# Attention and two MLPs on one core: a pair's P.V. behind the next pair's third scores, decay rows in one load, new order behind the first norm, no clip of weights

## The chip, the cores and the metric

The kernel runs on one core of a Trainium2 chip. The metric is device microseconds of one execution; the time before is the median of three executions. TensorE (PE) multiplies matrices, VectorE (DVE) and ScalarE (ACT) do the elementwise work, GpSimd (POOL) a little of it and some transfers, and SyncE (SP) issues most transfers (DMA), the transposing ones among them.

## The reference

There are 4 batches, 8 heads, 576 tokens and 64 columns per head; x has 512 columns.

```
scores = q @ k.T / sqrt(D); decay = cum[:, None] - cum[None, :]   # cum = cumsum(log f)
attn   = softmax(where(causal, -1e9, scores + decay))
x      = attn @ v                                   # heads side by side: B x S x 512
xn     = (x - mean) / sqrt(var + 1e-6) * g_ln
x      = x + relu(xn @ w_ch1) @ w_ch2               # 512 -> 2048 -> 512
h      = relu(x @ w_in); u, v = h[..., :512], h[..., 512:]
vs     = einsum('ts,bsd->btd', w_spatial, norm(v)) + b_spatial
out    = (u * vs) @ w_out
```

The weights arrive as 64-bit floats.

## The kernel before

The work is cut into token blocks. Blocks 0 and 1 hold the first 128 tokens of each batch (`attention32`, float32), blocks 2 and 3 the tokens 128 to 255 (`attention1`, lines 566 to 620), blocks 4 to 7 the tokens 256 to 575 of one batch each (`attention`, lines 623 to 675). Each block's x is then normalised (`norm`) and goes through the first MLP as part of one of the groups (`mlp`): for each of 16 hidden tiles j, PE forms `ph` (L909) from `xh`, `xl` and a weight tile, ACT makes `hh` of it (L920), DVE the remainder `hl` (L924), and PE adds into `acc` (L894). Operands are pairs of 16-bit halves, so that a product takes three matmuls. Group 0 works in float32 with the narrowed weights. Behind the first MLP comes the second, from about 500 us on.

`attention` takes a block's 8 heads as 4 pairs. A pair has three score tiles of 128 queries or 64: `weights(2)` with 384 keys, `weights(3)` with 512, `weights(4)` with 576 (cut into two of 288); here they are called first, second and third scores. For each, PE makes the scores `s` (L385), DVE adds the decay `D` and finds the maximum (L411, `sd`, `st`), ACT takes the exponential with its sum (L415, L417), ACT and DVE write the two halves of P (L331, L432), and SP issues a transposing DMA of P into `PT` (L435), two for each score tile, all on one queue in a fixed order. `values` (P.V.) then multiplies `PT` by `vp`, the two halves of v, with 30 matmuls (L635) into `av`, and ACT copies that out (L640, L641). The P.V. of a pair is issued in the loop of the next one: `late` keeps it. `operands` loads `qkz` (L354 to L358) and the decay rows `D` (L362) of a pair. P.V. of the fourth pair of a block has no next pair, and stands behind the loop.

The weight tiles are loaded as 64-bit words (`raw`, three buffers) and narrowed to 32 bits during group 0 (`load_w`, `narrow`: L704 and L705 on ACT, L706 to L708 on DVE; L706 clips the magnitude). Their squares go through PE (L758), `scales` makes two factors of the sums, and `make16` splits all 16 tiles into halves at the start of group 1 (L789 on ACT, L792 on DVE).

Generators of these pieces are stepped through by one list of events (positions in numbers such as `CONV`). What they emit goes through a scheduler, which fixes the order of each engine's instructions when the program is built; `self.after(a, b)` keeps a behind b in that order. On the chip each engine works through its list in order and waits where an operand isn't there.

Of the kernel before, what the change touches and what calls it, by code (L numbers as in the profile page):

```python
# [6 lines left out]
F32 = mybir.dt.float32  # L7
# [6 lines left out]
AF = mybir.ActivationFunctionType  # L14
ALU = mybir.AluOpType
# [3 lines left out]
P = 128  # L19
B, H, S, D = 4, 8, 576, 64  # L20
DM, DFF, DF2 = 512, 2048, 1024
NK = DM // P
NF = DFF // P
NP = H // 2
# [30 lines left out]
    SPAN.append((SPAN[-1][1], SPAN[-1][1] + 2.35 / 4))  # L55
SPAN.append((SPAN[-1][1] - 0.034, SPAN[-1][1] + 0.02))
RAWAT = (-0.975, -0.974, -0.973)
CONV = (-0.6, 0.001, 0.002, 0.003, 0.004)
PACE = (1, "x3", "split", "split", "split")
LOWAT = (1, "x3", "split")  # L60
SUMS = 14
REST = 0.35
SQ = (1, 3, 4, 5, 6, 8, 9, 10, 12, 13, 14, 16)
# [21 lines left out]
def words(raw, w, dt):  # L85

    return raw.bitcast(dt).rearrange("p (n w) -> p n w", w=2)[:, :, w]


class Kernel:  # L90
# [41 lines left out]
    def setup(self):  # L132
        nc, ctx = self.nc, self.ctx
        self.cst = ctx.enter_context(self.pool("cst"))
        self.dram = ctx.enter_context(self.tc.tile_pool(name="dram", bufs=1, space=DRAM))
        cst = self.cst
        self.onesf = cst.tile([P, P], F32, name="onesf")
        nc.vector.memset(self.onesf, 1.0 / DM)
        self.ones = cst.tile([P, P], F32, name="ones")
        nc.vector.memset(self.ones, 1.0)  # L140
        self.gT = cst.tile([P, NK], F32, name="gT")
        self.eps = cst.tile([P, 1], F32, name="eps")
        nc.vector.memset(self.eps, EPS)
        self.decay1_d = self.dram.tile([B * H, 2, 3 * P], F32, name="decay1_d")
        self.decay_d = self.dram.tile([B * H, S], F32, name="decay_d")
        self.xt_d = self.dram.tile([P, NK, B, S - 512], F32, name="xt_d")
        self.x2_d = self.dram.tile([DM, NT], F32, name="x2_d")

# [92 lines left out]
    def decays16(self):  # L241


        nc, cum, n = self.nc, self.cum, B * H
        dec1 = self.dec1
        ins = nc.scalar.activation(dec1[:, 0, :P], cum[:, P : 2 * P], AF.Copy, scale=8.0)
        self.after(ins, self.marks["x3"])
        self.after(nc.scalar.activation(dec1[:, 1, P:], cum[:, : 2 * P], AF.Copy, scale=-8.0), ins)
        nc.gpsimd.dma_start(out=self.decay1_d, in_=dec1)
        row = nc.vector.tensor_scalar(out=self.lg, in0=cum, scalar1=cum[:, MID : MID + 1], scalar2=-8.0, op0=ALU.subtract, op1=ALU.mult)  # L250
        self.after(row, self.joined)
        nc.gpsimd.dma_start(out=self.decay_d, in_=self.lg)

    def gscale(self):

        nc = self.nc
        g = self.at.tile([P, DM], F32, name="gall")
        m = self.cst.tile([P, 1], F32, name="gmax")
        self.gsc = self.cst.tile([P, 2, 1], F32, name="gsc")
        self.gs = self.cst.tile([P, NK], F32, name="gs")  # L260
        load = nc.gpsimd.dma_start(out=g, in_=self.moe_g_ln.rearrange("p k -> (p k)").partition_broadcast(P))
        self.after(load, self.marks["x3"])
        biggest = nc.vector.tensor_reduce(out=m, in_=g, axis=mybir.AxisListType.X, op=ALU.max, apply_absolute_value=True)
        self.after(biggest, self.marks["third"])
        nc.vector.tensor_tensor(out=m, in0=m, in1=m, op=ALU.mult)
        self.pow2(m, self.gsc, up=UPX, k=0)
        nc.vector.tensor_scalar(out=self.gs, in0=self.gT, scalar1=self.gsc[:, 1], scalar2=None, op0=ALU.mult)
# [9 lines left out]
    def parts16(self, v, h, l, b=None):  # L277


        nc, at = self.nc, self.at  # L280
        if b is None:
            ss = at.tile([P, 1], F32, tag="vq", name="vq", bufs=4)
            sm = at.tile([P, 2, 1], F32, tag="vs", name="vs", bufs=4)
            nc.scalar.activation(h, v, AF.Square, accum_out=ss)
            pn = self.bank("s")
            nc.tensor.matmul(pn[:, :1], lhsT=self.ones, rhs=ss, start=True, stop=True)
            self.pow2(pn[:, :1], sm)
            b = 0
        else:
            sm = self.vsc  # L290
        undo, scale = sm[:, 0, b : b + 1], sm[:, 1, b : b + 1]
        nc.scalar.activation(h, v, AF.Copy, scale=scale)
        nc.vector.scalar_tensor_tensor(out=l, in0=v, scalar=scale, in1=h, op0=ALU.mult, op1=ALU.subtract)
        return undo
# [46 lines left out]
    def operands(self, b, p):  # L341

        nc, at = self.nc, self.at
        W, C = QW + 64, QW + 64 + S
        if not self.qkz:
            for i in range(BUFS["qk"]):
                self.qkz.append(at.tile([P, C], F32, name=f"qkz{i}"))
                for u in range(2):
                    c = 3 * P - 64 - 64 * u
                    nc.gpsimd.memset(self.qkz[i][64 * u : 64 * u + 64, c : c + 64], 0.0)  # L350
        qk = self.qkz[0]
        self.qkz.append(self.qkz.pop(0))
        src = self.pair_of(b)[p]
        nc.sync.dma_start(out=qk[:, W:], in_=src[:, QW:])  # L354
        nc.sync.dma_start(out=qk[:, : 2 * P], in_=src[:, : 2 * P])
        for u in range(2):
            us, c = slice(64 * u, 64 * u + 64), 2 * P + 64 * u
            nc.sync.dma_start(out=qk[us, c : c + 64], in_=src[us, 2 * P : QW])  # L358
        decay = at.tile([P, 2, S], F32, tag="D", name="D", bufs=BUFS["D"])
        r = b // 2 * 2 * H + 4 * p + b % 2  # L360
        for u in range(2):
            nc.sync.dma_start(out=decay[:, u], in_=self.decay_d[r + 2 * u].partition_broadcast(P))  # L362
        xh = at.tile([P, C], F32R, tag="xh", name="xqh", bufs=BUFS["xh"])
        xl = at.tile([P, C], F32R, tag="xl", name="xql", bufs=BUFS["xl"])
        for c in (slice(0, W), slice(W, C)):
            nc.scalar.activation(xh[:, c], qk[:, c], AF.Copy)
            nc.vector.tensor_tensor(out=xl[:, c], in0=qk[:, c], in1=f32(xh[:, c]), op=ALU.subtract)
        return xh, xl, decay
# [80 lines left out]
    def attention32(self, b, xT):  # L449
# [34 lines left out]
        def scores(p):  # L484
# [9 lines left out]
            for n, u, c in four_:  # L494
# [4 lines left out]
                ex = nc.scalar.activation(e[:, n, u], e[:, n, u], AF.Exp, bias=mn, scale=-1.0, accum_out=sm)  # L499
                if b:  # L500
                    self.after(masked, self.marks["third" if p else "w1"])
                    self.after(ex, self.marks["split"])
                if not b and p == NP - 1:
                    self.after(masked, self.drawn)
            if not b:
# [21 lines left out]
        for p in range(NP):  # L527
            for i in range(len(ahead), min(p + 2, NP) if b else NP):
# [1 line left out]
                    ahead[0] = norms(*ahead[0])  # L530
                ahead.append(scores(i))
                yield
            if b or p:
                ahead[p] = norms(*ahead[p])
            e, diag = ahead[p]
            ps, pt = bank(tags[1]), four("PT")
# [1 line left out]
                ins = mm(ps[:, n, u], lhsT=e[:, n, u], rhs=diag[:, n, u], start=True, stop=True, skip_group_check=True)  # L538
            if not b and p < NP - 1:
                self.fill(FILLS[2], ins)  # L540
            if b or p % 2:
                copied = nc.scalar.activation(pt, ps, AF.Copy)
            else:
                copied = nc.vector.tensor_copy(out=pt, in_=ps)
            if not b:
                self.done.append(copied)
                self.marks[f"PT{p}"] = copied
# [72 lines left out]
    def attention(self, b, xT, xt):  # L620
# [28 lines left out]
        for p in range(NP):  # L649
# [3 lines left out]
            yield  # L653
            if p + 1 < NP:
                ops = self.operands(b, p + 1)
            if late:
                values(*late, self.done_low)
            yield
            vr = at.tile([P, 5, P], F32, tag="vr", name="vr", bufs=BUFS["vr"])
            nc.sync.dma_start(out=vr, in_=self.v[b, :, p * P : (p + 1) * P].rearrange("(t p) d -> p t d", p=P))  # L660
            yield from self.weights(3, heads)
            yield
            vp = at.tile([P, 2, 5, P], F16, tag="vp", name="vp", bufs=BUFS["vp"])
            yield from self.weights(4, heads)
            vsc = self.parts16(vr, vp[:, 0], vp[:, 1], b)
# [25 lines left out]
    def narrow(self, raw, tmp, low=None, behind=None):  # L691
# [9 lines left out]
            nc.vector.scalar_tensor_tensor(out=b, in0=lo, scalar=29, in1=b, op0=ALU.logical_shift_right, op1=ALU.bitwise_or)  # L701
        else:

            first = nc.scalar.activation(a, words(raw, 1, F32), AF.Abs, scale=2.0**16)  # L704
            self.low = nc.scalar.activation(low.bitcast(I32), lo, AF.Copy, scale=LOW)  # L705
            clip = nc.vector.tensor_scalar(out=a, in0=a, scalar1=F64_LO * 2.0**16, scalar2=F64_HI * 2.0**16, op0=ALU.max, op1=ALU.min)  # L706
            sign = nc.vector.scalar_tensor_tensor(out=low, in0=hi, scalar=0x80000000, in1=low, op0=ALU.bitwise_and, op1=ALU.bitwise_or)
            self.joined = nc.vector.scalar_tensor_tensor(out=b, in0=b, scalar=3, in1=low, op0=ALU.logical_shift_left, op1=ALU.bitwise_or)  # L708
            if behind is not None:
                if behind is not self.marks["PT2"]:  # L710
                    self.after(clip, behind)
                self.after(sign, behind)
        return first

# [90 lines left out]
    def norm(self, x, s, y, whole, end, c):  # L805
# [33 lines left out]
            pv = self.mean(tag, sq[:, 0])  # L839
        t1 = ns.tile([P, TOK], F32, tag="t1", name="t1", bufs=2)  # L840
        nc.scalar.activation(y, pv, AF.Ln, bias=self.eps)
        nc.scalar.activation(y, y, AF.Exp, scale=-0.5)
        nc.vector.scalar_tensor_tensor(out=t1, in0=pv, scalar=EPS, in1=y, op0=ALU.add, op1=ALU.mult)
        nc.vector.scalar_tensor_tensor(out=t1, in0=t1, scalar=-0.5, in1=y, op0=ALU.mult, op1=ALU.mult)
        nc.vector.scalar_tensor_tensor(out=y, in0=t1, scalar=1.5, in1=y, op0=ALU.add, op1=ALU.mult)
# [400 lines left out]
    def run(self):  # L1246
# [85 lines left out]
            events += [(a0 + (a1 - a0) * (e + 0.5) / steps[n], 1, n) for e in range(steps[n])]  # L1332
        for g, (b0, b1) in enumerate(zip(BEGIN, BEGIN[1:])):
            events += [(b0 + (b1 - b0) * (e + 0.01) / (NF + 1), 0, g) for e in range(NF + 1)]
        events += [(CONV[j] if j < len(CONV) else G1 * (j - len(CONV) + 0.5) / (NF + 1), -1, j) for j in range(NF)]
        events += [(MAKE + 0.001 * j if j < SOON else G1 + 0.5 * (j - SOON + 0.5) / (NF + 1), -1, NF + 2 + j) for j in range(NF)]
        events += [(WSC, -1, NF + 1)] + [(VN + 0.04 * i, -1, NF) for i in range(B + 2)]
        events += [(at, -2, j) for j, at in enumerate(RAWAT)] + [(REST, -1, -1), (DEC, -1, -2)]
# [152 lines left out]
```

## Time and profile before

| | |
|---|---|
| median of 3 executions | 805.84 us (805.52 to 806.53) |
| the profiled execution | 802.58 us; its span 800.8 us, 1.78 us lie around it |
| PE busy | 760.3 us, 95% of the span |
| DVE, ACT, POOL busy | 554.3, 501.8, 66.8 us |
| PE's granted clock, mean | 0.993 of full speed |
| bytes moved | 105.96 MB, 132 GB/s |

The span runs from the first instruction to the last of the profiled execution. An engine's busy time is the sum of its instructions; PE's counts matmuls whose ends are modelled, and which overlap where they follow each other. [...]

### The profile page before, as it was taken

Reading aid. Unit: us, or ns where it says so; the run is one execution under the profiler, and the core shown is the slowest. Engines: PE = TensorE matmul, PEld = TensorE weight load, DVE = VectorE, ACT = ScalarE, POOL = GpSimd, SP = SyncE. Lnnn points to the kernel's source line nnn. Section 1 sums busy time; section 2 is a strip of 40 time slices with the busy share of each in tenths; the row PEclk is TensorE's granted clock in tenths of the full one; section 3 lists DMA queues with packets and bytes.
Section 4 is the critical chain, followed back from the end, with each engine's and each line's share of the span. In section 5 each row is a group of like instructions: output and inputs, shape, how many; then the busy total and the mean of one; then the engine's idle time right before and its main releaser. Section 6 shows DMA issues by size and latency. Waiting matters only on the chain.

```text
span 800.8 us, 16517 instructions
## 1 busy us (share of the span) xinstructions
PE 760.3 (95%) x6142; PEld 576.9 (72%) x6142; DVE 554.3 (69%) x1508; ACT 501.8 (63%) x1251; POOL 66.8 (8%) x109
## 2 busy tenths in 40 slices
PE   7899997999989999899899999999999999999998
PEld 6789886878867777688678788644447667668676
DVE  7989799485578779678877873778535562654634
ACT  6887598485477677576766763567325744656543
POOL 5000111012101011001101100100012000000000
PEclk9999999999999999999999999999999999999999
DMA  9968893376678888968996775552015230000101
GB/s 261 297 229 275 250 191 67 80 161 108 197 152 170 168 207 157 168 152 176 224 170 156 126 112 149 149 162 80 1 31 95 87 99 1 31 31 1 60 1 60
DMA packets 170963, 105.96 MB, mean 132 GB/s; under 512 B 109090, under 2 KB 156290, under 8 KB 170884
## 3 DMA queue, kind: packets, MB, share of 16 engines
q1 hardware_dynamic: 164696, 98.24, 50.7%
q0 software_dynamic: 5328, 5.16, 5.0%
q10 hardware_dynamic: 860, 1.52, 0.6%
q8 instruction: 48, 0.79, 0.4%
q14 instruction: 31, 0.25, 0.1%
HBM read 66.01 MB, written 14.72 MB: 101 GB/s over the span
## 4 chain that ended last, share of the span: by engine, by line
PE 53%; ACT 12%; DVE 12%; DMA 11%; issue 9%; SPq 1%; POOL 0%; ACTq 0%; DVEq 0%; POOLq 0%
PE ph L909 10%; PE acc L894 8%; PE pb L854 8%; PE pb L855 7%; PE pb L853 7%; DMA PT<-P 5%; PE av L635 2%; ACT wt L789 2%; DVE P L432 2%; DVE sd L411 2%; PE s L385 2%; ACT P L331 2%; DMA vr<-in_v_dram 2%; PE s L894 1%; ACT sd L415 1%
## 5 line engine op out<-in xcount | busy, mean ns | idle before, releaser
L894 PE MATMUL acc<-hh,wt 128*128 128x256 f16 (+2 forms) x960 | 197.0, 296 | 2.5 <-ACT hh L920 2.3
L909 PE MATMUL ph<-xh,wt 128*128 128x256 f16 (+1 forms) x896 | 186.8, 290 | 5.5 <-DVE hl L924 5.3
L909 PEld LDWEIGHTS <-wt 128*128 128x128 f16 x1344 | 129.4, 99 | 48.0 <-issue 10.4
L894 PEld LDWEIGHTS <-wt 128*128 128x128 f16 x1344 | 129.6, 98 | 44.0 <-issue 6.1
L909 PE MATMUL ph<-xl,wt 128*128 128x256 f16 (+1 forms) x448 | 129.5, 290 | 0.0
L894 PE MATMUL acc<-hl,wt 128*128 128x256 f16 (+1 forms) x416 | 116.0, 282 | 1.7 <-DVE hl L924 1.7
L331 ACT ACTIVATE P<-sd,st 128x384 f16<-128x384 f32 (+2 forms) x128 | 68.8, 586 | 26.1 <-DVE st L418 17.5
L920 ACT ACTIVATE hh<-ph 128x256 f16<-128x256 f32 (+2 forms) x128 | 51.0, 399 | 51.0 <-PE ph L909 50.8
L924 DVE SCALAR_TENSOR_TENSOR hl<-ph,hh 128x256 f16<-128x256 f32 (+1 forms) x112 | 51.0, 458 | 42.9 <-ACT hh L920 41.5
L415 ACT ACTIVATE sd<-sd,st 128x384 f32<-128x384 f32 (+2 forms) x80 | 54.7, 684 | 38.1 <-DVE st L411 37.9
L432 DVE SCALAR_TENSOR_TENSOR P<-sd,st,P 128x512 f16<-128x512 f32 (+1 forms) x96 | 58.2, 633 | 16.7 <-ACT P L331 15.9
L411 DVE CUSTOM_DVE_ANT_0 sd<-s,D 128x384 f32<-128x384 f32 (+2 forms) x96 | 52.4, 563 | 7.2 <-PE s L385 6.4
L945 POOL DMA_DIRECT2D x_d<-t x36 | 31.8, 1062 | 205.7 <-DVE t L941 172.3
L635 PE MATMUL av<-PT,vp 128*64 128x320 f16 (+2 forms) x480 | 32.6, 276 | 11.6 <-DMA PT<-P 11.6
L635 PEld LDWEIGHTS <-vp 128*64 128x64 f16 x480 | 25.8, 113 | 20.6 <-issue 13.0
L1221 DVE SCALAR_TENSOR_TENSOR u<-pb,wsc,u 128x288 f32<-128x288 f32 x32 | 16.0, 514 | 34.5 <-PE pb L1220 34.5
L853 PE MATMUL pb<-x2h,wil 128*128 128x288 f16 (+2 forms) x144 | 37.8, 273 | 0.0
L854 PE MATMUL pb<-x2l,wih 128*128 128x288 f16 (+2 forms) x144 | 37.7, 273 | 0.0
L855 PE MATMUL pb<-x2h,wih 128*128 128x288 f16 (+2 forms) x144 | 37.7, 273 | 0.0
L853 PE MATMUL pb<-wsh,vl 128*128 128x288 f16 x128 | 36.6, 286 | 0.2
L855 PE MATMUL pb<-wsh,vh 128*128 128x288 f16 x128 | 36.6, 286 | 0.0
L854 PE MATMUL pb<-wsl,vh 128*128 128x288 f16 x128 | 36.6, 286 | 0.0
(308 smaller groups left out, 1632.2 us busy)
## 6 DMA issues: line engine op xcount, KB each, us to landing
raw<-in_moe_w_ch_dram SPq DMA_DIRECT2D x32, 512.0 KB
D<-decay_d SPq DMA_DIRECT2D x32, 288.0 KB
vraw<-in_v_dram SPq DMA_DIRECT2D x5, 1024.0 KB
vr<-in_v_dram SPq DMA_DIRECT2D x16, 320.0 KB
x_d<-xT SPq DMA_DIRECT2D x9, 512.0 KB
x_d<-t POOLq DMA_DIRECT2D x36, 128.0 KB, 4.7
qkz<-in_qk_dram SPq DMA_DIRECT2D x16, 288.0 KB
out_dram<-o SPq DMA_DIRECT2D x32, 144.0 KB
```

Source lines behind the costliest of these rows:

```text
L331: self.nc.scalar.activation(out, in_, AF.Copy, scale=scale)
L411: self.marks["seen"] = nc.vector.tensor_tensor_reduce(out=sd[us, c0:c1], in0=banks[n if both else w][us, : c1 - c0], in1=decay[us, u, c0:c ...
L415: nc.scalar.activation(sd[:, :N], sd[:, :N], AF.Exp, bias=st[:, c : c + 1], scale=-1.0, accum_out=st[:, 4 + w : 5 + w])
L432: low = nc.vector.scalar_tensor_tensor(out=dl, in0=src, scalar=rs, in1=dh, op0=ALU.mult, op1=ALU.subtract)
L635: ins = nc.tensor.matmul(pav[us, n0:W], lhsT=vp[:, vi, kt, us], rhs=heads[u][1][:, 2 * kt + pi, n0:W], start=(kt == 0 and (vi, pi) == (0, ...
L853: first = mm(out, lhsT=al, rhs=bh, start=start, stop=False, **kw)
L854: mm(out, lhsT=ah, rhs=bl, start=False, stop=False, **kw)
L855: mm(out, lhsT=ah, rhs=bh, start=False, stop=stop, **kw)
L894: ins = nc.tensor.matmul(acc[m], lhsT=a, rhs=b, start=bank not in clear, stop=last and e == len(terms) - 1, skip_group_check=True)
L909: ins = nc.tensor.matmul(ph, lhsT=a, rhs=b, start=k == e == 0, stop=k == NK - 1 and e == len(terms) - 1)
L920: relu = nc.scalar.activation(hh, ph, AF.Relu)
L924: nc.vector.scalar_tensor_tensor(out=hl, in0=ph, scalar=0.0, in1=hh, op0=ALU.max, op1=ALU.subtract)
```

## The change

In `attention` the call of `values` for the pair before moves from ahead of `weights(3)` to behind it, so that the scheduler places it behind the third scores. In `operands` the two decay loads of a pair become one, from a table laid out by pairs. `attention1` of block 2, whose v is squared first (`b is None` in `parts16`), keeps these squares behind the last normalisation's exponential (`self.spread`, L842). The events of the weight tiles 3 and 4 and of the later ones, and the anchors that ACT's part of `narrow` stands behind (`PACE`, `LOWAT`), are other numbers. In `attention32` the norms of block 0's next pair come ahead of the copies of PT. `narrow` loses its clip L706 in the branch for the first MLP's weights; the scale of L704 becomes 2^-112 in place of 2^16.

```diff
-CONV = (-0.6, 0.001, 0.002, 0.003, 0.004)
-PACE = (1, "x3", "split", "split", "split")
-LOWAT = (1, "x3", "split")
+CONV = (-0.6, 0.001, 0.002, 0.06, 0.061)
+PACE = (1, "x3", "split", NP + 1, NP + 1)
+LOWAT = (1, "x3", "split", NP + 1, NP + 1)
@@ parts16
-            nc.scalar.activation(h, v, AF.Square, accum_out=ss)
+            self.after(nc.scalar.activation(h, v, AF.Square, accum_out=ss), self.spread)
@@ operands
-        r = b // 2 * 2 * H + 4 * p + b % 2
-        for u in range(2):
-            nc.sync.dma_start(out=decay[:, u], in_=self.decay_d[r + 2 * u].partition_broadcast(P))
+        rows = self.decay_d[b // 2 * NP + p, b % 2].rearrange("u s -> (u s)").partition_broadcast(P)
+        nc.sync.dma_start(out=decay.rearrange("p u s -> p (u s)"), in_=rows)
@@ attention32
-            if b or p:
+            if b:
                 ahead[p] = norms(*ahead[p])
...
             if not b and p < NP - 1:
                 self.fill(FILLS[2], ins)
+                ahead[p + 1] = norms(*ahead[p + 1])
@@ attention
-            if late:
-                values(*late, self.done_low)
             yield
             vr = at.tile([P, 5, P], F32, tag="vr", name="vr", bufs=BUFS["vr"])
...
             yield from self.weights(3, heads)
             yield
+            if late:
+                values(*late, self.done_low)
@@ narrow
-            first = nc.scalar.activation(a, words(raw, 1, F32), AF.Abs, scale=2.0**16)
+            first = nc.scalar.activation(a, words(raw, 1, F32), AF.Abs, scale=2.0**-112)
...
-            clip = nc.vector.tensor_scalar(out=a, in0=a, scalar1=F64_LO * 2.0**16, scalar2=F64_HI * 2.0**16, op0=ALU.max, op1=ALU.min)
...
-                if behind is not self.marks["PT2"]:
-                    self.after(clip, behind)
@@ norm
-        nc.scalar.activation(y, y, AF.Exp, scale=-0.5)
+        self.spread = nc.scalar.activation(y, y, AF.Exp, scale=-0.5)
```

PE, block 4, around the P.V. of its first pair, which is called in the loop of the second. Before, the last matmuls of that P.V. (`av`) stand straight ahead of the third scores (288 columns):

```order
L635 LDWEIGHTS vp
L635 MATMUL av<-PT,vp 64x64
L385 MATMUL s<-xqh,xql 128x288
L385 MATMUL s<-xql,xqh 128x288
L385 MATMUL s<-xqh 128x288
L385 MATMUL s_2846<-xqh,xql 128x288
L385 MATMUL s_2846<-xql,xqh 128x288
L385 LDWEIGHTS ident_1692
L385 MATMUL s_2846<-far,ident_1692 128x64
L385 MATMUL s_2846<-xqh 128x288
```

Now they stand ahead of the first scores (384 columns) of the pair after, with three matmuls of `acc` between; the third scores are 21 matmuls of `acc` ahead of the P.V.:

```order
L637 LDWEIGHTS vp
L637 MATMUL av<-PT,vp 64x64
L893 LDWEIGHTS wt
L893 MATMUL acc<-hh,wt 128x256
L893 LDWEIGHTS wt
L893 MATMUL acc<-hl,wt 128x256
L893 LDWEIGHTS wt
L893 MATMUL acc<-hh,wt 128x256
L385 MATMUL s_2885<-xqh,xql 128x384
L385 MATMUL s<-xqh,xql 128x384
```

So the third scores no longer follow the P.V., and the next pair's first scores do. ACT one pair later, before: the copies of `av` come behind the P of the second scores (`4x128`), and ahead of the next operands (L366) and of the third scores' exponential (L415, 576 columns) and P:

```order
L331 ACTIVATE P_3095<-sd,st 128x4x128
L640 ACTIVATE xT<-av,vsc 128x256
L641 ACTIVATE xt<-av,vsc 128x64
L292 ACTIVATE vp<-vr,vsc 128x640
L366 ACTIVATE xqh<-qkz_2383 128x384
L366 ACTIVATE xqh<-qkz_2383 128x576
L920 ACTIVATE hh<-ph 128x256
L415 ACTIVATE sd,st<-sd,st 128x576
L417 ACTIVATE st<-st 128x1
L331 ACTIVATE P_3118<-sd,st 128x4x128
L331 ACTIVATE P_3118<-sd,st 128x64
```

And now:

```order
L366 ACTIVATE xqh<-qkz_2367 128x384
L366 ACTIVATE xqh<-qkz_2367 128x576
L415 ACTIVATE sd,st<-sd,st 128x576
L417 ACTIVATE st<-st 128x1
L332 ACTIVATE P_3098<-sd,st 128x4x128
L642 ACTIVATE xT<-av,vsc 128x256
L643 ACTIVATE xt<-av,vsc 128x64
L332 ACTIVATE P_3098<-sd,st 128x64
L293 ACTIVATE vp<-vr,vsc 128x640
L919 ACTIVATE hh<-ph 128x256
```

The copies of `av` have moved behind the third scores' exponential, into the middle of its P. ACT near the end of group 0, before: the squares of block 2's v (L284) stand around the exponential of a norm (L842), the first exponentials of `attention1` (L590) right behind them:

```order
L920 ACTIVATE hh<-ph 128x256
L284 ACTIVATE vp,vq<-vr 128x256
L841 ACTIVATE y<-av,eps 128x256
L284 ACTIVATE vp,vq<-vr 128x256
L842 ACTIVATE y<-y 128x256
L284 ACTIVATE vp,vq<-vr 128x256
L292 ACTIVATE vp<-vr,vs 128x256
L590 ACTIVATE sd,st<-sd,st 128x256 x2
```

Now the squares follow the exponential of the second norm, after the 16-bit splits of four weight tiles (L788) and ahead of group 1's `xh`:

```order
L919 ACTIVATE hh<-ph 128x256
L841 ACTIVATE y<-y 128x256
L285 ACTIVATE vp,vq<-vr 128x256 x3
L788 ACTIVATE wt<-wt,w1c 128x512
L788 ACTIVATE wt<-wt,w2c 128x512
L919 ACTIVATE hh<-ph 128x256
L871 ACTIVATE xh<-xT,gs 128x256 x4
```

The attention of block 2 has moved from the end of group 0 into the start of group 1. On SP a pair's loads change their order (the one `D` load after the first of `qkz`, `vr` last), and the six transposes of a pair keep theirs. From the last P.V. on, PE's order is the same in both.

## Rows read from the trace of the kernel before

**Rows 1.** The page: busy us of each engine (share of the span), instructions.

```profile
PE 760.3 (95%) x6142; PEld 576.9 (72%) x6142; DVE 554.3 (69%) x1508; ACT 501.8 (63%) x1251; POOL 66.8 (8%) x109
```

**Rows 2.** PE's waits: line, what was waited for, us in total, times, longest.

```profile
PE av L635 <- DMA PT<-P: 11.6, 11, 2.2
PE ph L909 <- DVE hl L924: 5.3, 7, 1.7
...
PE s L583 <- DMA qk<-in_qk_dram: 2.0, 1, 2.0
PE s L385 <- DVE st L411: 1.7, 2, 1.0
```

**Rows 3.** Windows, PE: us, PE busy (count), granted clock, DMA share, GB/s.

```profile
117.00:200.00 83.00, 76.64 (x730) 0.98 0.55 105
...
225.00:490.00 265.00, 248.31 (x2379) 0.99 0.83 161
490.00:615.00 125.00, 124.58 (x699) 1.00 0.40 104
...
385.00:400.00 15.00, 11.88 (x119) 1.00 1.14 217
```

**Rows 4.** Timeline of PE, P.V.: start, us, instruction, idle before.

```profile
254.78 0.30 PE L635 MATMUL av<-PT,vp 128*64 128x320 f16 x1 [1.77 <-DMA PT<-P]
...
285.56 0.30 PE L635 MATMUL av<-PT,vp 128*64 128x320 f16 x1 [0.18 <-DMA PT<-P]
...
323.55 0.30 PE L635 MATMUL av<-PT,vp 128*64 128x320 f16 x1 [2.18 <-DMA PT<-P]
...
420.56 0.30 PE L635 MATMUL av<-PT,vp 128*64 128x320 f16 x1 [1.25 <-DMA PT<-P]
...
486.10 0.30 PE L635 MATMUL av<-PT,vp 128*64 128x320 f16 x1 [0.39 <-DMA PT<-P]
```

**Rows 5.** Windows of PE behind the wait at 323.55.

```profile
323.00:325.00 2.00, 1.45 (x9) 0.95 1.29 254
325.00:327.00 2.00, 2.00 (x16) 0.50 0.06 13
327.00:329.00 2.00, 2.00 (x26) 0.70 0.77 149
```

**Rows 6.** Timeline of PE: one matmul, and two that follow each other.

```profile
319.79 0.27 PE L894 MATMUL acc<-hl,wt 128*128 128x256 f16 x1
319.89 0.38 PE L894 MATMUL acc<-hh,wt 128*128 128x256 f16 x2
```

**Rows 7.** Timeline of ACT behind a P.V.

```profile
257.78 0.48 ACT L640 ACTIVATE xT<-av,vsc 128x256 f32<-128x256 f32 x1
258.15 0.31 ACT L641 ACTIVATE xt<-av,vsc 128x64 f32<-128x64 f32 x1
258.35 0.83 ACT L292 ACTIVATE vp<-vr,vsc 128x640 f16<-128x640 f32 x1
```

**Rows 8.** Timeline of SP's queue: transposes of a pair, and the next decay loads.

```profile
249.99 10.53 SPq L435 DMA_TRANSPOSE PT<-P  x6
...
261.81 1.03 SPq L362 DMA_DIRECT2D D<-decay_d  x2
```

**Rows 9.** Line 706, the clip: count, shortest/median/longest ns, first and last start.

```profile
L706 DVE TENSOR_SCALAR wt<-wt x17: 416/686/1690, 18.4 to 81.8; 128x1024 f32<-128x1024 f32 x15, 128x512 f32<-128x512 f32 x2
```

**Rows 10.** Line 284 and ACT's timeline, from block 2's squares to group 2.

```profile
L284 ACT ACTIVATE vp<-vr x8: 405/407/417, 86.4 to 143.5; 128x256 f16<-128x256 f32 x8
...
109.15 0.41 ACT L842 ACTIVATE y<-y 128x256 f32<-128x256 f32 x1
...
156.32 0.37 ACT L609 ACTIVATE xT<-av,vs 128x128 f32<-128x128 f32 x1 [0.52 <-PE av L608]
...
178.20 1.70 ACT L872 ACTIVATE xh<-xT,gs 128x256 f16<-128x256 f32 x4
```

**Rows 11.** Window of all engines at the start of group 1: PE, PEld, DVE, ACT, POOL.

```profile
100.00:130.00 30.00, 25.66 (x235) 22.09 (x234) 29.49 (x75) 28.98 (x74) 7.41 (x12) 1.00 0.76 150
```

More of the change, by code (lines that the diff above doesn't have):

```diff
@@ L144, in setup @@
         self.decay1_d = self.dram.tile([B * H, 2, 3 * P], F32, name="decay1_d")
-        self.decay_d = self.dram.tile([B * H, S], F32, name="decay_d")
+        self.decay_d = self.dram.tile([B // 2 * NP, 2, 2, S], F32, name="decay_d")
         self.xt_d = self.dram.tile([P, NK, B, S - 512], F32, name="xt_d")
@@ L251, in decays16 @@
         self.after(row, self.joined)
-        nc.gpsimd.dma_start(out=self.decay_d, in_=self.lg)
+        for i in range(2):
+            nc.gpsimd.dma_start(out=self.decay_d[:, i], in_=self.lg[i::2])
     def gscale(self):
@@ L263, in gscale @@
         biggest = nc.vector.tensor_reduce(out=m, in_=g, axis=mybir.AxisListType.X, op=ALU.max, apply_absolute_value=True)
-        self.after(biggest, self.marks["third"])
+        self.after(biggest, self.joined)
         nc.vector.tensor_tensor(out=m, in0=m, in1=m, op=ALU.mult)
@@ L501, in scores @@
                     self.after(masked, self.marks["third" if p else "w1"])
-                    self.after(ex, self.marks["split"])
+                    self.after(ex, self.done[-1])
                 if not b and p == NP - 1:
@@ L544, in attention32 @@
                 copied = nc.vector.tensor_copy(out=pt, in_=ps)
+                self.after(copied, self.masked)
             if not b:
@@ L1334, in run @@
             events += [(b0 + (b1 - b0) * (e + 0.01) / (NF + 1), 0, g) for e in range(NF + 1)]
-        events += [(CONV[j] if j < len(CONV) else G1 * (j - len(CONV) + 0.5) / (NF + 1), -1, j) for j in range(NF)]
+        events += [(CONV[j] if j < len(CONV) else max(0.061 + 0.0001 * j, G1 * (j - len(CONV) + 0.5) / (NF + 1)), -1, j) for j in range(NF)]
         events += [(MAKE + 0.001 * j if j < SOON else G1 + 0.5 * (j - SOON + 0.5) / (NF + 1), -1, NF + 2 + j) for j in range(NF)]
```

## The prediction

> **What bounds the kernel now.** I read the page's busy times first. PE is busy 760.3 of 800.8 us, DVE 554.3, ACT 501.8 [rows 1]. So a change pays where PE stands still, or where it takes work from PE, and this one takes no matmul away. The second view is PE's waits by line: the largest is that of the P.V. (L635) for the transposed P, 11 times and 11.6 us, the longest 2.2 us; then group 1's and later groups' `ph` for `hl`, 5.3 us; then single waits of some 2 us [rows 2]. The third is PE by windows: from 225 to 490 us, while the blocks 4 to 7 run, PE is idle 265 - 248.3 = 16.7 us; from 490 to 615 us, behind the last P.V., it is idle 0.4 us [rows 3]. So the wait named largest is the one that the moved P.V. can shorten, and everything behind it comes forward by as much, since PE is then full. The fourth is the timeline, where each wait has its place: those of the fourth pairs of a block (at 285.56, 420.56 and 486.10 us) last 0.18, 1.25 and 0.39 us, together 1.82; the others include the longest, 2.18 us at 323.55, and 1.77 us at 254.78 [rows 4].
>
> **The moved P.V.** The P.V. of the first three pairs of each of 4 blocks moves, 12 in all; the fourth pairs' have no next pair and stay. So 8 of the 11 waits can go, with 11.6 - 1.82 = 9.8 us [rows 2, 4]. How much later does PE now come to them? At the place shown in PE's order the third scores and 21 matmuls of `acc` are now ahead of it. Matmuls of 256 columns follow each other at 0.11 us: one alone takes 0.27 us, two take 0.38 [rows 6]. So 21 of them are 2.3 us, and the third scores, six of 288 columns at 0.11 x 288/256 = 0.12 and two small ones, about 0.8 us: 3.1 us more, and at the other eleven places 3 to 5.5 us by the same count. The transposes that it waits for become later too: the P of the third scores is now cut in two by the copies of `av`, 0.48 + 0.31 = 0.8 us [rows 7]. The margin of 3.1 - 0.8 = 2.3 us is just above the longest wait, so I take all 8 as gone: **-9.8 us**.
>
> Each wait also costs PE its overlap: the matmul ahead of it runs out its 0.27 us instead of 0.11 [rows 6], so 8 x 0.16 = **-1.3 us**. And behind the longest one the granted clock falls: 0.50 (1.2 GHz) for 2 us and 0.70 for 2 us more, after 0.95 [rows 5]; the work lost is 2 x 0.50 + 2 x 0.30 + 2 x 0.05 = 1.7 us at the full 2.4 GHz. Behind the waits up to 1.77 us no such stretch follows that I found. Without the 2.18 us wait: **-1.7 us**.
>
> **What becomes late instead.** The next pair's first scores now follow the third ones with 24 matmuls of `acc` and 30 of P.V. between. They need a bank of `s`, which DVE frees (L411). Such waits stand in the trace already: two, 1.7 us together, the longer 1.0, so the shorter 0.7 [rows 2]. None of the 12 new places need wait (0), or each like the shorter (8.4 us). I take a third of them, 4 x 0.7 = **+2.8 us**, since 24 x 0.11 + 30 matmuls of up to 320 columns leave DVE over 4 us for its four reads.
>
> Behind a fourth pair's third scores the P.V. stays close, and their P too is now cut by the copies of the third pair's `av`. Three of the four wait already [rows 4], so a delay there is paid in full: up to 4 x 0.8 = 3.2 us [rows 7], at least 0. Part of the copies runs while ACT would wait for DVE; I take a third, **+1.0 us**.
>
> **The decay rows.** 16 loads replace 32 of the same bytes; two took SP 1.03 us [rows 8], so SP gains about 0.5 us a pair. No wait of PE names D [rows 2], and a pair's six transposes alone hold the queue 10.5 us [rows 8]: 0, and at most 12 x 0.5 = 6 us if SP's queue were what makes the transposes late. [...]
>
> **The clip.** 17 instructions on DVE, 15 x 0.69 + 2 x 0.42 = 11.2 us, all between 18 and 82 us [rows 9]. They lie under PE's float32 group 0, which waits for the data of tiles and for ACT there; if the cover were gone they would be worth at most their 11.2 us. Taken as 0, with the reordered copies and tiles of that stretch.
>
> **Block 2's squares.** The first stood at 86.4 us; now they follow the second norm's exponential, at 109.15 us in the old trace [rows 10]. DVE and ACT are full in that stretch, 29.5 and 29.0 of 30 us [rows 11], so group 1 starts sooner when block 2's first three score tiles leave it: about 4 us, an estimate from counting DVE's instructions up to the first `hl`. But group 2 can't start before block 2 is through: its last copy is at 156.32 us, and `xh` for group 2 starts at 178.20 [rows 10]. In ACT's new order that copy stands behind 13 hidden tiles of group 1, where it stood behind 11; a hidden tile is 24 matmuls on PE, 2.6 us by rows 6. So 2 x 2.6 - 4 = 1.2 us later, against which the wait for `qk` of 2.0 us [rows 2] gets shorter, as that load now stands one transpose earlier on SP's queue. I take **0**, with bounds of -4 and +5.2.
>
> **Sum.** -9.8 - 1.3 - 1.7 + 2.8 + 1.0 = **-9.0 us** against the profiled 802.58 us: 793.6. The median before is 805.84, 3.3 us above the profiled execution, and I carry that over: **796.8 us**. By the bounds of the terms without the front: 805.84 - 12.8 = 793.0 and 805.84 - 12.8 + 8.4 + 3.2 = 804.6.
>
> **The rivals.**
>
> *The front gains too.* Group 1 keeps its 4 us and block 2 ends as early as before it. For it: the window of rows 11, and PE's waits of 5.3 us for `hl` and 2.0 for `qk` [rows 2], part of which go. Against it: the old 22 us from the last copy to `xh` [rows 10] are a chain of their own. Time: 796.8 - 4 = 792.8 us.
>
> *The wait only moves.* The transposes come at the pace of DMA and of SP's queue, and the P.V. meets them at its new place, or the first scores take over. For it: the DMA share is 0.83 over the 265 us and 1.14 around the waits at 389 and 392 [rows 3], 1.29 at 323 [rows 5]; at 0.83 x 265 = 220 us the transfers have a floor 45 us below, but in the stretches that count they are at it. Against it: the P.V. comes 3 us later than its data needs. Time: half to none of the gain, 801 to 806, in the middle 803.5 us. [...]
>
> *Block 2 comes late.* It is the one that ends slower. Its eight score tiles took from 86.4 to 156.3 us, 69.9 us [rows 10]. If they keep that pace from the new start, 109.15 - 4 = 105.2, the last copy comes at 175.1, 18.8 us later, and PE stands before group 2 with nothing left of group 1: 805.84 + 18.8 - 9.0 = 815.6 us. It decides from the point where that copy comes more than 9 us late, at 165.3 us. For it: few buffers, and a transpose and a P.V. in each round. Against it: in the old order 16 weight splits on ACT and DVE lay between these rounds [rows 11], and in the new one most come first.
>
> **How the numbers follow.** 0.2%, or 1.6 us, is about what a measurement of this kernel can tell from no change: 804.2 to 807.5 us. The forecast has 0.58, the front's gain 0.13, the wait that moves 0.16, block 2 late 0.13. Faster: 0.57 + 0.13 + 0.06 of the third = 0.76. Same: 0.01 + 0.10 + 0.02 of the last = 0.13. Slower: 0.11. From 789 to 805 us lie nearly all of the first two cases and most of the third, 0.81.
>
> **What would show it.** Right: PE's wait for the transposed P falls to some 3 us, all of it in fourth pairs; PE's idle time from the first scores of block 4 to the last P.V. falls from 16.7 to some 9 us; no stretch at 0.50 there; waits of the first scores for L411 rise to about 4.5 us. The front: the first `hl` of group 1 about 4 us earlier, group 2's `xh` still near 178 us. Wrong if the P.V. still waits in first to third pairs by more than 5 us together, if L411 is waited for by more than 9 us, or if group 2's `xh` moves by more than 5 us either way; a faster kernel whose P.V. waits stand unchanged would be right by accident.

## The result, and the profile after

The changed kernel takes 798.12 us (median of 8 executions, 795.07 to 799.49); the kernel before 806.18 us (median of 8, 800.35 to 808.88). The ratio is 0.990, with a 95% interval of 0.987 to 0.993. The forecast was 796.8 us. The profiled execution took 799.43 us; it is among the slower of the eight, where the profiled one of before (802.58 us) was among the faster, so the two traces differ by 3.2 us only. In what follows they say where PE waits; what an edit is worth is taken from the ratios.

The page of the changed kernel, busy us of each engine:

```profile
PE 764.0 (96%) x6142; PEld 579.3 (73%) x6142; DVE 543.1 (68%) x1491; ACT 500.3 (63%) x1251; POOL 69.4 (9%) x110
```

DVE is 11.2 us lighter than in [rows 1], which is the clip. PE's waits of the changed kernel:

```profile
PE s L385 <- DVE st L411: 8.5, 9, 2.1
PE av L610 <- DMA PT<-P: 4.2, 2, 3.2
PE av L637 <- DMA PT<-P: 3.3, 4, 1.2
PE s L585 <- DMA qk<-decay_d: 2.5, 1, 2.5
...
PE ph L908 <- DVE hl L923: 2.1, 4, 1.0
```

Against [rows 2] the P.V.'s wait for the transposed P (now L637) has gone from 11.6 us in 11 to 3.3 in 4, and these four are the fourth pairs, which didn't move. The scores' wait for the maxima L411 has grown from 1.7 us in 2 to 8.5 in 9: six of the nine stand at first scores, 7.4 us together, where one of 0.7 stood, and three at third scores, 1.1 us, where one of 1.0 stood. In `attention1` the P.V. (L610) now waits 4.2 us for the transposed P, the longest of all PE's waits, 3.2 us, among them; before it was 0.7. Windows of PE (us, PE busy, granted clock, DMA share, GB/s):

```profile
117.00:200.00 83.00, 76.48 (x676) 0.90 0.61 117
225.00:490.00 265.00, 251.37 (x2430) 0.99 0.82 163
...
120.00:128.00 8.00, 8.00 (x37) 0.50 0.63 93
...
184.00:188.00 4.00, 3.96 (x33) 0.50 0.81 120
...
392.00:394.00 2.00, 2.00 (x12) 0.50 1.25 267
```

From 225 to 490 us PE is idle 13.6 us, where it was 16.7 [rows 3]. The stretch ahead of it is new: from 117 to 200 us the granted clock is 0.90, where it was 0.98, and 8 us of it are wholly at 0.50 (matmuls of 256 columns start 0.21 us apart from 120.04 to 122.36 us, and 0.11 apart at 1.00, from 130.07 to 133.02), behind the wait of 3.2 us, and 4 us more behind the wait of 2.5 us for `qk`. The waits, and the longest of the later stages:

```profile
119.25 0.85 PE L610 MATMUL av<-PT,vp 128*64 128x128 f16 x12 [3.20 <-DMA PT<-P]
...
349.22 0.32 PE L637 MATMUL av<-PT,vp 128*64 128x320 f16 x1 [1.23 <-DMA PT<-P]
...
390.29 0.45 PE L385 MATMUL s<-xqh,xql 64*128 64x384 f32 x2 [2.10 <-DVE st L411]
```

The second line is the longest wait of a fourth pair, the third the longest of the first scores. Behind the last one the clock falls again, as it did behind the P.V.'s 2.18 us in [rows 4, 5]: the stretch at 0.50 has moved with the wait. ACT's timeline shows block 2 (beginning, last copy) and `xh` of groups 1 and 2:

```profile
98.75 0.41 ACT L841 ACTIVATE y<-y 128x256 f32<-128x256 f32 x1
99.06 0.41 ACT L285 ACTIVATE vp<-vr 128x256 f16<-128x256 f32 x1
...
101.96 1.71 ACT L871 ACTIVATE xh<-xT,gs 128x256 f16<-128x256 f32 x4
...
161.63 0.37 ACT L611 ACTIVATE xT<-av,vs 128x128 f32<-128x128 f32 x1 [0.62 <-PE av L610]
...
182.69 1.70 ACT L871 ACTIVATE xh<-xT,gs 128x256 f16<-128x256 f32 x4
```

Against [rows 10] block 2's first square comes 12.7 us later, its last copy 5.3, and group 2 starts 4.5 us later, although group 1's `xh` comes some 10 us sooner (first line at 112.5 us in the trace before).

### The profile page after: what moved, and what is told of

Read it like the earlier page. It is cut to its first block, busy times and chain, and to the rows that moved or that the text cites. A ratio compares the mean times of both kernels' runs of the same rounds, so it can differ in the third digit from the quotient of the medians.

```text
span 797.7 us, 16458 instructions
## 1 busy us (share of the span) xinstructions
PE 764.0 (96%) x6142; PEld 579.3 (73%) x6142; DVE 543.1 (68%) x1491; ACT 500.3 (63%) x1251; POOL 69.4 (9%) x110
## 4 chain that ended last, share of the span: by engine, by line
PE 51%; DVE 17%; ACT 11%; DMA 10%; issue 10%; SPq 1%; POOL 0%; ACTq 0%; DVEq 0%; POOLq 0%
PE ph L908 9%; PE pb L853 8%; PE pb L854 8%; PE pb L852 8%; PE acc L893 8%; DVE sd L411 4%; DVE P L432 3%; DMA PT<-P 3%; ACT sd L415 3%; ACT P L332 2%; DMA qkz<-in_qk_dram 2%; DVE wt L791 1%; PE s L893 1%; DMA raw<-in_moe_w_in_dram 1%; DVE xql L367 1%
## 5 line engine op out<-in xcount | busy, mean ns | idle before, releaser
L908 PE MATMUL ph<-xh,wt 128*128 128x256 f16 (+1 forms) x896 | 190.2, 294 | 2.3 <-DVE hl L923 2.1
L908 PE MATMUL ph<-xl,wt 128*128 128x256 f16 (+1 forms) x448 | 131.2, 293 | 0.0
L415 ACT ACTIVATE sd<-sd,st 128x384 f32<-128x384 f32 (+2 forms) x80 | 54.7, 685 | 51.2 <-DVE st L411 51.0
L432 DVE SCALAR_TENSOR_TENSOR P<-sd,st,P 128x512 f16<-128x512 f32 (+1 forms) x96 | 58.3, 631 | 18.1 <-ACT P L332 17.3
L411 DVE CUSTOM_DVE_ANT_0 sd<-s,D 128x384 f32<-128x384 f32 (+2 forms) x96 | 52.1, 563 | 3.5 <-PE s L385 2.8
L853 PE MATMUL pb<-gl,woh 128*128 128x288 f16 x128 | 35.6, 286 | 0.1
L854 PE MATMUL pb<-gh,woh 128*128 128x288 f16 x128 | 35.5, 286 | 0.0
```

The source lines that it names most:

```text
L411: self.marks["seen"] = nc.vector.tensor_tensor_reduce(out=sd[us, c0:c1], in0=banks[n if both else w][us, : c1 - c0], in1=decay[us, u, c0:c ...
L415: nc.scalar.activation(sd[:, :N], sd[:, :N], AF.Exp, bias=st[:, c : c + 1], scale=-1.0, accum_out=st[:, 4 + w : 5 + w])
L432: low = nc.vector.scalar_tensor_tensor(out=dl, in0=src, scalar=rs, in1=dh, op0=ALU.mult, op1=ALU.subtract)
L853: mm(out, lhsT=ah, rhs=bl, start=False, stop=False, **kw)
L854: mm(out, lhsT=ah, rhs=bh, start=False, stop=stop, **kw)
L908: ins = nc.tensor.matmul(ph, lhsT=a, rhs=b, start=k == e == 0, stop=k == NK - 1 and e == len(terms) - 1)
```

## The experiments

All ratios are to the kernel before, timed in the same session; the intervals are of 95%. The changed kernel stands at 0.990.

**1. The moved P.V. alone (e1).** On the kernel before, only the call moves:

```diff
-            if late:
-                values(*late, self.done_low)
             yield
...
             yield from self.weights(3, heads)
             yield
+            if late:
+                values(*late, self.done_low)
```

> The kernel before with the moved P.V. alone. Theory A (the move makes the gain, the rest is near nothing): 7 to 9 us below the kernel before, 797 to 799 us; P.V. waits for the transposed P fall from 11.6 us to about 3.3 us, waits of first scores for L411 rise from 1.7 us to about 8.5. Theory B (the L411 waits eat most of the move, and the front makes the other half): 3 to 5 us below, 801 to 803 us, with the same two waits. Up to the first scores of block 4 the trace is that of the kernel before under both.

797.82 us, 0.9934 (0.9904 to 0.9964): 5.3 us below the kernel before, between the two theories. Its waits:

```profile
PE s L385 <- DVE st L411: 8.9, 9, 2.1
PE av L635 <- DMA PT<-P: 5.5, 4, 3.3
```

The move takes 6.1 us from the P.V. and gives 7.2 to the scores, so by these two lines alone it gains nothing. The four P.V. waits left are fourth pairs; the longest, 3.3 us, had been 1.3 [rows 4]. In the two profiled executions the first score matmul of block 4 comes at 210.1 us before and at 206.7 here, with the same order up to there, and the last P.V. matmul at 489.1 and 484.2: of the 4.9 us between them 3.4 lie ahead of the moved work, where single executions differ by as much without a change, and 1.5 behind. So the ratio's 5.3 us (2.9 to 7.7 by its interval) is not all seen as waits in the trace, and my sum of 9.0 was too large.

**2. The P.V. back in the changed kernel (e2).** The same lines the other way.

> The changed kernel with the P.V. back in its old place. Theory A: within 2 us of the kernel before, 804 to 807 us, P.V. waits near 11 us again. Theory B: 3 to 5 us below the kernel before, 801 to 803 us.

807.28 us, 1.0053 (1.0025 to 1.0080): slower than the kernel before. So in the changed kernel the move is worth 1.5%, some 12 us, where alone it is worth 5.3. The trace shows one part of that, a longer wait in the old place:

```profile
PE av L637 <- DMA PT<-P: 15.9, 11, 4.6
```

Why it is longer there than the 11.6 us of [rows 2] these runs don't settle.

**3 and 4. Block 2's squares (e3, e4).** One takes the rule out of the changed kernel, the other puts it alone into the kernel before:

```diff
-            self.after(nc.scalar.activation(h, v, AF.Square, accum_out=ss), self.spread)
+            nc.scalar.activation(h, v, AF.Square, accum_out=ss)
```

> The changed kernel with block 2's squares free again, not behind the norm's exponential. Theory A: within 1.5 us of the changed kernel. Theory B: 2 to 4 us slower than the changed kernel. A third one, C (the late block 2 costs: a 3.2 us wait for its transposes at 119 us, 10 us at 0.50 behind it, group 2 4.5 us later): 3 to 5 us faster than the changed kernel, and group 2's xh back near 178 us.

> The kernel before with block 2's squares behind the norm's exponential, and nothing else. Theory A: within 1.5 us of the kernel before. Theory B: 2 to 4 us faster. C: 2 to 5 us slower, with group 2's xh at 180 to 185 us instead of 178.

Without the rule: 789.07 us, 0.9827 (0.9789 to 0.9865), about 6 us by the ratios below the changed kernel. The rule alone: 807.04 us, 1.0047 (1.0023 to 1.0072), 3.8 us above the kernel before. Theory C holds on both sides; without the rule the gain is even above its 3 to 5 us. ACT's timeline without the rule (e3), last copy of block 2 and `xh` of group 2:

```profile
153.85 0.37 ACT L611 ACTIVATE xT<-av,vs 128x128 f32<-128x128 f32 x1 [1.50 <-PE av L610]
...
175.24 1.71 ACT L871 ACTIVATE xh<-xT,gs 128x256 f16<-128x256 f32 x4
```

And with the rule alone (e4):

```profile
180.88 1.70 ACT L872 ACTIVATE xh<-xT,gs 128x256 f16<-128x256 f32 x4
```

Group 2 starts at 175.2, 178.2 [rows 10], 180.9 and 182.7 us: without the rule, before, with the rule alone, in the changed kernel. In e3 the window that stood at 0.90 in the changed kernel is at 1.00; with the rule alone (e4) it is at 0.96, before at 0.98 [rows 3]:

```profile
117.00:200.00 83.00, 80.88 (x785) 1.00 0.53 113
```

**5 to 7. What else the change holds (e5, e6, e7).** All three on e3: the clip back (with the scale 2^16 and its place in the order), the old numbers of the weight tiles, and two decay loads:

```diff
...
+            clip = nc.vector.tensor_scalar(out=a, in0=a, scalar1=F64_LO * 2.0**16, scalar2=F64_HI * 2.0**16, op0=ALU.max, op1=ALU.min)
...
```

```diff
-CONV = (-0.6, 0.001, 0.002, 0.06, 0.061)
+CONV = (-0.6, 0.001, 0.002, 0.003, 0.004)
...
```

```diff
-        rows = self.decay_d[b // 2 * NP + p, b % 2].rearrange("u s -> (u s)").partition_broadcast(P)
-        nc.sync.dma_start(out=decay.rearrange("p u s -> p (u s)"), in_=rows)
+        for u in range(2):
+            nc.sync.dma_start(out=decay[:, u], in_=self.decay_d[b // 2 * NP + p, b % 2, u].partition_broadcast(P))
```

> The changed kernel without the rule on block 2's squares (789.1 us), and with the clip back. Theory C1 (the clip's 11 us of DVE lay ahead of group 1 and its absence brings the front forward): 793 to 797 us, group 1's xh 3 to 4 us later than 107.8 us. C2 and C3 (it is the order of the weight tiles, or the joined decay loads): within 1.5 us of 789.

> The same base with the old events and anchors of the weight tiles (CONV, PACE, LOWAT, the max in the events). C2 (the new order of the tiles brings the front forward): 793 to 797 us, group 1's xh 3 to 4 us later than 107.8 us. C1 and C3: within 1.5 us of 789.

> The same base with two decay loads of a pair again. C3 (half as many loads on SP's queue bring the transposes forward): 792 to 795 us, P.V. waits and waits of the first scores for L411 grow by 2 us or more together. My prediction's 0: within 1.5 us of 789, the same waits.

The old tile numbers: 789.01 us, 0.9824 (0.9794 to 0.9855), no difference. The clip: 792.62 us, 0.9870 (0.9832 to 0.9909), about 3.5 us slower, though the interval meets that of e3; and C1's sign for it is not there, as `xh` of group 1 doesn't come later (107.8 us in e3):

```profile
106.72 1.70 ACT L874 ACTIVATE xh<-xT,gs 128x256 f16<-128x256 f32 x4
```

Two loads: 794.82 us, 0.9893 (0.9862 to 0.9925), about 5 us slower; the interval is apart from that of experiment 6 in the same session. The waits of e7:

```profile
PE s L385 <- DVE st L411: 9.0, 8, 2.1
PE av L637 <- DMA PT<-P: 4.6, 4, 2.0
```

and of e3:

```profile
PE s L385 <- DVE st L411: 8.2, 8, 2.1
...
PE av L637 <- DMA PT<-P: 3.2, 4, 1.2
```

The two waits together are 2.2 us longer, as C3 had it; that is less than half of the 5 us.

**8. The remainder of the operands on GpSimd (e8).**

```diff
-            nc.vector.tensor_tensor(out=xl[:, c], in0=qk[:, c], in1=f32(xh[:, c]), op=ALU.subtract)
+            nc.gpsimd.tensor_tensor(out=xl[:, c], in0=qk[:, c], in1=f32(xh[:, c]), op=ALU.subtract)
```

> The same base with the remainder of the next pair's operands (L367, 1.3 us a pair) on GpSimd instead of VectorE. Theory D (VectorE's work between a pair's third scores and the next pair's first is what those wait for): waits of the first scores for L411 fall from 8.2 to under 4 us and the time by 3 to 6 us, 783 to 786 us. Rival E (GpSimd is slower at it, and the first scores wait for xql instead): the sum of both waits stays, 788 to 792 us.

799.12 us, 0.9958 (0.9930 to 0.9986), slower than both theories had it. The waits for L411 stay (7.8 us), 1.5 us for `xql` are added, `ph` waits 5.5 us for `hl` where it waited 2.5 in e3, and some of DVE's instructions slow down beside GpSimd's work:

```profile
365.81 3.44 POOL L367 TENSOR_TENSOR xql<-qkz,xqh 128x384 fp32r<-128x384 f32 x2 [2.17 <-ACT xqh L366]
...
...
367.91 1.89 DVE L432 SCALAR_TENSOR_TENSOR P<-sd,st,P 128x512 f16<-128x512 f32 x1
```

L432 with 512 columns takes 760 ns on average in e3 from 225 to 490 us and 903 here; this one takes 1.89 us beside GpSimd's two of 3.44 together. So the experiment doesn't show what these waits would be with L367 off DVE and DVE as fast as before.

**9 and 10. Joined loads and no clip, each with the moved P.V. on the kernel before (e9, e10).** The edits are those of the change.

> The kernel before with the moved P.V. and the joined decay loads, nothing else. If the joined loads are worth 5 us wherever they stand (theory L): 0.986 to 0.989 of the kernel before, against 0.9934 with the moved P.V. alone; P.V. waits and L411 waits together 2 us or more below the 14.4 us of that one. If they are worth nothing, as I had put it: 0.992 to 0.995.

> The kernel before with the moved P.V. and without the clip, nothing else. If VectorE's 11 us of clip delay the start of group 1 (theory K): 0.988 to 0.991 of the kernel before, and group 1's xh before 109 us instead of 111.3. If the clip lies under PE's work, as I had put it: 0.992 to 0.995 and the same xh.

The loads: 795.24 us, 0.9896 (0.9854 to 0.9939), 3 us below e1, with intervals that overlap; its profiled execution, 802.97 us, was the slowest of six by 5.7 us and doesn't serve for waits. No clip: 792.22 us, 0.9843 (0.9805 to 0.9880), 7 us below e1, with intervals apart, and below the range of theory K too. `xh` of groups 1 and 2 in e10:

```profile
93.93 0.91 ACT L869 ACTIVATE xh<-xT,gs 128x256 f16<-128x256 f32 x2 [0.49 <-DVE xT L844]
...
166.55 0.91 ACT L869 ACTIVATE xh<-xT,gs 128x256 f16<-128x256 f32 x2
```

and in e1:

```profile
111.26 1.71 ACT L872 ACTIVATE xh<-xT,gs 128x256 f16<-128x256 f32 x4 [0.78 <-DVE xT L847]
...
176.91 1.71 ACT L872 ACTIVATE xh<-xT,gs 128x256 f16<-128x256 f32 x4
```

Without the clip group 1 is ready 17 us earlier and group 2 10 us, more than the clip's own 11.2 us [rows 9] explain for group 1: the scheduler also places what stood around it anew.

**11. The second scores' remainder behind the third maxima (e11).** On e3:

```diff
+            if both:
+                self.after(self.done_low, self.marks["seen"])
```

> The changed kernel without the rule on block 2's squares (0.9827), and VectorE's last remainder of the second scores' P (L432, 0.75 us a pair) ordered behind the maxima of the third scores (L411). Theory D (VectorE's order ahead of those maxima makes the first scores wait): the waits for L411 fall from 8.2 us to 2 to 4 us, 0.977 to 0.980 of the kernel before, if the later transposes of the second scores don't take it back; P.V. waits up by at most 2 us. Rival (the wait comes from elsewhere): unchanged waits, 0.981 to 0.985.

796.26 us, 0.9890 (0.9853 to 0.9927): slower than e3. The waits say where it went:

```profile
PE ph L910 <- DVE hl L925: 5.3, 8, 1.4
PE av L639 <- DMA PT<-P: 4.1, 3, 3.4
...
PE s L385 <- DVE st L411: 2.3, 5, 0.7
PE av L639 <- DMA qkz<-in_qk_dram: 2.1, 1, 2.1
```

Theory D is right about the cause, since the waits for L411 fall from 8.2 to 2.3 us with DVE's order alone. But P.V. and the next `hl` take all of it back: 5.3 us for `hl` against 2.5 in e3, and 6.2 for the P.V. by these two lines against 3.2. That leaves no gain; why it is some 5 us slower than e3 these lines don't show.

**12. Without the explicit dependency between score tiles (e12).** On e3:

```diff
-            elif "seen" in self.marks:
-                self.after(ins, self.marks["seen"], mybir.DependencyClass.Sync)
```

> The same base without the explicit dependency of each score tile's first matmul on the last maximum of the tile before; the buffers alone order them. Theory S (the first scores' own banks are free after the earlier maxima, and only this dependency holds them): waits for L411 fall below 3 us, 0.976 to 0.980. Theory D (VectorE is late with the remainder L367 of the operands too): the wait moves to xql or to a bank, 0.981 to 0.985.

798.05 us, 0.9916 (0.9888 to 0.9945): 7 us slower than e3, though the wait is nearly gone:

```profile
PE av L635 <- DMA PT<-P: 7.8, 4, 2.9
...
PE s L385 <- DVE st L409: 0.9, 1, 0.9
```

The two profiled executions took 792.66 us (the fastest of nine) and 792.53 in e3 (the slowest of six), so the traces show what was exchanged, and not the 7 us. The waits for L411 fall from 8.2 to 0.9 us, but the P.V.'s rise from 3.2 to 7.8, and PE is busier, 764.8 us against 758.7. By groups, 225 to 490 us (busy us, mean ns of one), e12:

```profile
L385 PE MATMUL s<-xqh,xql 64*128 64x512 f32 x28 | 10.8, 492 | 0.9 <-DVE st L409 0.9
...
L385 PE MATMUL s<-xqh,xql 64*128 64x384 f32 x28 | 10.4, 448 | 0.0
```

and e3:

```profile
L385 PE MATMUL s<-xqh,xql 64*128 64x512 f32 x30 | 7.5, 497 | 1.0 <-DVE st L411 0.9
...
L385 PE MATMUL s<-xqh,xql 64*128 64x384 f32 x28 | 6.2, 434 | 6.8 <-DVE st L411 6.8
```

The means are alike, and the busy time differs: the two heads of a pair, 64 rows each, lie beside each other on PE when their matmuls alternate, as here in e3, two in 0.45 us:

```profile
237.38 0.45 PE L385 MATMUL s<-xqh,xql 64*128 64x384 f32 x2 [1.34 <-DVE st L411]
```

In e12 one head's first matmul starts when its own bank is free, matmuls of the MLP come between, and the two no longer run together:

```profile
233.65 0.50 PE L385 MATMUL s<-xqh,xql 64*128 64x512 f32 x1
234.08 0.39 PE L891 MATMUL acc<-hh,wt 128*128 128x256 f16 x2
235.34 0.50 PE L385 MATMUL s<-xqh,xql 64*128 64x512 f32 x1 [0.86 <-DVE st L409]
```

So the dependency that causes the wait also keeps the heads together; neither theory had that.

## Why the prediction was right, and where its steps were not

The time came within 1.4 us of the forecast and inside its range; its direction and the place named first were right, but several terms were off and cancelled, so that it came this close is in part luck. Of the signs, the P.V.'s waits came as foretold. PE's idle time in blocks 4 to 7 fell to 13.6 us and not to some 9, the waits for L411 rose to 8.5 us and not 4.5, just under the 9 that would have meant wrong, and a stretch at 0.50 was there again. By the experiments, what the later scores took back was made up by terms put at nothing, the clip and the decay rows.

**The moved P.V., -9.8 us.** Right in mechanism and in size: the eight waits of the moved pairs are gone in the trace, and what is left, 3.3 us, is in the four fourth pairs, as foretold. There the forecast added 1.0 us to 1.8; 1.5 were added.

**The overlap, -1.3 us.** If each wait costs PE its overlap, the number of waits counts, and that didn't fall: 11 of the P.V. and 2 of the scores before, 4 and 9 now. By this count nothing is left of the term.

**What becomes late instead, +2.8 us.** This is the term that was mis-sized: 8.5 us in place of 1.7, so +6.8. I let a third of the twelve places wait, at the shortest old wait, 0.7 us; six first scores wait, 1.2 us on average and up to 2.1. (Of the two old waits only that of 0.7 stood at first scores; the longer, 1.0, stood at third ones.) The four microseconds that I granted DVE for "its four reads" aren't free. From 386.15 us on, ahead of the longest wait, its timeline in the changed kernel is

```profile
386.15 0.44 DVE L411 CUSTOM_DVE_ANT_0 sd<-s,D 64x288 f32<-64x288 f32 x1
...
386.63 0.46 DVE L411 CUSTOM_DVE_ANT_0 sd<-s,D 64x288 f32<-64x288 f32 x1
...
387.14 0.75 DVE L432 SCALAR_TENSOR_TENSOR P<-sd,st,P 128x512 f16<-128x512 f32 x1
387.81 0.55 DVE L367 TENSOR_TENSOR xql<-qkz,xqh 128x384 fp32r<-128x384 f32 x1
388.39 0.51 DVE L411 CUSTOM_DVE_ANT_0 sd<-s,D,st 64x288 f32<-64x288 f32 x1
...
388.83 0.75 DVE L367 TENSOR_TENSOR xql<-qkz,xqh 128x576 fp32r<-128x576 f32 x1
389.61 0.52 DVE L411 CUSTOM_DVE_ANT_0 sd<-s,D,st 64x288 f32<-64x288 f32 x1
```

with a remainder of P and both of the next operands between the four reads, 2.05 us. Experiment 11, which puts the remainder of P alone behind these reads, takes 5.9 of 8.2 us from the waits; what the operands' share is, no run shows alone.

**The clock, -1.7 us.** The traces give the clock as a share of full speed and not in GHz; the term needs the share alone. The stretch behind the P.V.'s wait went, and another came behind the first scores' 2.10 us wait. Zero net in that place; and behind the 3.2 us wait of block 2 the chip granted 0.50 for 8 us, 4 us of work lost, which no term held. Over the whole stretch from 117 to 200 us, 0.90 in place of 0.98 is 6.6 us of work at the full clock in these two executions.

**Block 2's squares, 0.** Wrong: they cost 3.8 us alone and about 6 in the changed kernel (experiments 3 and 4). The step that failed is the balance "2 x 2.6 - 4 = 1.2 us later". Group 1 did gain, its first `hl` coming at 117.6 us instead of 124.2; but group 2 came 4.5 us late, because block 2's rounds ran out into a wait for their own transposes and the low clock behind it. That is the rival that ends slower, in part: the last copy came at 161.6 us, on the near side of the 165.3 us from which it would have decided.

**The clip and the decay rows, 0 each.** Wrong too, in the other direction. The clip's absence is worth about 3.5 us (experiment 5, not resolved) to 7 (experiment 10). Its cover was real in group 0, where PE waits 1.3 us for narrowed tiles before and 0.3 after, but what stands behind it on DVE is the way to group 1's `xh`, and the scheduler fills the room. That is how experiment 10 is read here; experiment 5, where `xh` doesn't come later with the clip, doesn't show it. The joined loads are worth some 3 to 5 us (experiments 9 and 7), near the 6 us that I had given as the bound if SP's queue made the transposes late. That no wait of PE names `D` was no reason for zero. That the loads delay what follows them on the queue fits the P.V.'s longer waits (4.6 us against 3.2), but no run shows the queue alone. The waits account for 2.2 us of it; the rest is not placed.

**What the clock's record adds.** The mean granted clock of every execution is on record. Its medians in one session are 0.993 before, 0.988 with the squares' rule alone (e4), 0.983 with the P.V. back (e2) and 0.9965 without the rule (e3); the changed kernel had 0.989. As an estimate, 0.005 of 805 us is 4 us of work at the full clock, and the rule alone costs 3.8; from 0.9965 to 0.989 it is 6 us, and the rule costs about 6 in the changed kernel; and 5 of the 12 us of experiment 2 would be the clock. In the next session it is 0.9925 with two loads (e7) and 0.9955 in e6, 2.4 of some 5 us. So much of these prices may be paid as low clock behind waits and not as the waits themselves. No run holds the clock fixed, so this is an agreement of numbers and not shown.

**The pace of DMA.** From 392 to 394 us, at a DMA share of 1.25, the core moved 267 GB/s in mixed traffic, where it was 217 at a share of 1.14 in [rows 3]. The P.V. of the fourth pairs still waits 3.3 us for the transposed P and block 2's 4.2 us, but such a wait holds the time until P is written too, and no run shows the transposes' pace apart.

Where the time lies shows in three marks of each profiled execution (one execution each, so good to a few us): the first score matmul of block 4, the last P.V. matmul, and the us between.

| kernel | first scores | last P.V. | between |
|---|---|---|---|
| before | 210.1 | 489.1 | 279.0 |
| changed | 211.2 | 487.2 | 276.0 |
| P.V. alone (e1) | 206.7 | 484.2 | 277.5 |
| changed, P.V. back (e2) | 208.3 | 492.0 | 283.7 |
| changed, no rule on squares (e3) | 204.2 | 478.6 | 274.4 |
| squares alone (e4) | 213.0 | 494.8 | 281.8 |
| P.V. and no clip (e10) | 198.6 | 475.6 | 277.0 |

The clip's absence shows in the first column (8.1 us from e1 to e10); the squares too (7.0 us in the changed kernel, 2.9 alone, where the last column has as much again). The P.V. shows in the last, by 1.5 us alone and 7.7 in the changed kernel. The joined loads show in neither by more than 1.1 us (e7 has 205.3, 480.5 and 275.2, against e3). By the ratios the sum would be -5.3 for the moved P.V. with its new waits, -3.5 to -7 for the clip, -3 to -5 for the loads, and +4 to +6 for the squares: -6 to -13, against the 8 measured. The terms are not independent: in experiment 2 the same rest without the moved P.V. brings nothing. Beyond the clock's share of it, why stays open, as does the effect of the other reordering in the first blocks, which was not tried alone.

The version to keep is the change without the rule on the squares: 789.07 us, 0.9827 of the kernel before (0.9789 to 0.9865), below the whole interval of the changed kernel.

## What to carry to other kernels

When work is moved from between two steps of an in-order engine, price the next wait by listing what the other engines hold between those steps, instruction by instruction, and not by a share of the waits already there. An instruction that no wait names can still cost (here the clip some 3.5 to 7 us): what is queued behind it on its engine or its queue has to be followed to the stage that starts there. Before moving a block's start to make room for another, follow the block to its end, and to what starts behind that.

## What the runs showed of the hardware that was not expected

GpSimd's elementwise work slowed some of VectorE's instructions down: in experiment 8 the 20 of L432 with 512 columns that overlap L367 on GpSimd took 1.11 us on average, single ones up to 1.9, the 28 others 0.79, and 0.76 was the mean without (e3). Beside the same work the reads L411 of 288 columns took 0.49 us (0.48 otherwise) and `hl` 0.42 (0.42), so not all of VectorE slows down. Two matmuls of 64 rows each, one head's on partitions 0 to 63 and the other's on 64 to 127, ran beside each other here while they alternated in PE's order (two in 0.45 us in experiment 3): the same products cost 10.4 instead of 6.2 us, busy time of 28, once others came between (experiment 12). And a granted clock of 0.50 lasted over 8 us in one stretch of the changed kernel, behind a wait of 3.2 us, and over 4 us behind one of 2.5; but behind a wait of 3.3 us in experiment 1, at 410.0 us, the granted clock was 0.89, 0.50 and 0.75 in three windows of 2 us, so the length of the wait alone doesn't tell how long it lasts.
